# A fused linear-attention and gated-convolution kernel: query units over half the sequence, more transposing transfers, and a new written-out order

## The chip, the cores and the metric

The kernel runs on one core of a Trainium2 chip. The metric is device time in microseconds. The engines are TensorE (PE; its weight loads are listed apart as PEld), VectorE (DVE), ScalarE (ACT), GpSimd (POOL) and SyncE (SP, which here only issues transfers). Each engine takes its instructions strictly in order and waits for others on semaphores.

## The reference

Eight batches, eight heads, a sequence of 576, head size 64, 128 random features. Linear attention first, then a gated causal convolution block over the 512 columns that the heads make together:

```python
def phi(x):                                   # used for q and for k
    proj = np.einsum('bhsd,df->bhsf', x, w_phi)
    proj = proj - np.max(np.abs(proj), axis=-1, keepdims=True)
    return np.concatenate([np.exp(proj), np.exp(-proj)], axis=-1)
kv  = np.einsum('bhsf,bhsd->bhfd', k_p, v);   z = np.sum(k_p, axis=2)
num = np.einsum('bhsf,bhfd->bhsd', q_p, kv)
den = np.einsum('bhsf,bhf->bhs', q_p, z)[..., None] + 1e-06
x   = (num / den)                             # to [B, S, H*D]
for k in range(5):                            # causal: rows s-4 .. s
    gate_pre += conv_w[k] * xp[:, k:k + S, :]
out = (sigmoid(gate_pre) * (x @ w_val)) @ w_out
```

Inputs and output are float32; inside, the kernel works in bfloat16 with sums in float32 in PSUM.

## The kernel before

**Units.** For one batch, q (or k) is laid on 128 partitions with 18 blocks of 128 columns. A q partition stands for a head, a half of the sequence ("run", 288 rows) and one of eight places in it; a column block holds an even and an odd row of each partition. `UNITS` cuts the 18 blocks into four units of four blocks and one of two. Everything on k and q goes by unit: project (TensorE), take the maxima of the absolute values (VectorE, `amax`, L585), take both exponentials (ScalarE, `kexp` L595, `qexp` L706 and L709).

**One batch** runs through these steps, by the kinds that the plan gives them:

- `kp`, `kmax`, `kexp`: projected k, its maxima MK, the exponentials KTIL. `ek` makes EK from the maxima (ScalarE), and `vs` makes VT, v times EK (POOL, L610). `st` sums KTIL times VT over the sequence (TensorE, L620), `kv` evicts the sum.
- `qm`, `qmax`: projected q and its maxima MQP. `mqt` and `mqr` transpose and negate them to MQR. `rx` spreads MQR over an identity pattern to RX, so that a matmul with ones can subtract the maxima in PSUM. `qp` projects q again with features on partitions and adds RX (L693, L698); `qexp` writes QTIL.
- `num` (L719, L726), `nrm` (reciprocal and product, VectorE, L737 and L740, to XN), then the transpose of XN to XT: `xtp` on TensorE with the copy `xtc` (L748, L628/L632), or, for the batches in `XB`, a transposing transfer by SP (`xtd`, L755).
- `gate` (the convolution as matmuls, L781), `tanh` (ScalarE), `val` (L791), `gv` (VectorE, L797), `out` (L813, L817), `oev` (evict), `odma` (store).

**The start.** k and q of batch 0 come as float32 in nine loads by SP into the spare space of KTIL (`load32`); TensorE transposes them (`tp32`, L536) and ScalarE or VectorE casts them out of PSUM (`tc32`, L542, L544). Batch 1's k and q are loaded by POOL as bfloat16 and transposed on TensorE. From batch 2 on they are loaded by POOL and transposed by a transfer that SP issues (`xpose`, L565). `hold` is a tiny POOL copy that makes POOL's later loads wait for a first load of batch 0.

**The order.** Nothing is scheduled when the program is built. `build` lists 1062 tasks with their dependencies, and `ORDER` gives the order in which their instructions are written out; each engine runs its part of it in that order. `FLEX` says, for each task that has a choice of engine, which one it takes; `BANKS` gives the PSUM banks. `WARM` and `ZERO` put matmuls without use between tasks, to keep TensorE busy. The durations in `build` are the planner's own and play no part when the program runs.

Of the kernel before, what the change touches and what calls it, by code (L numbers as in the profile page):

```python
# [27 lines left out]
XB = (6, 7)  # L28
# [6 lines left out]
WARM = (  # L35
    "60:6:1 81:1:1 87:7:2 134:7:1 141:7:1 "
)
ZERO = "35:76:7 61:80:5 75:34:1 101:105:1 118:99:1 126:215:8 144:223:1 155:192:4 158:200:1 175:315:6 189:346:1 195:241:2 197:241:2 211:327:1"
# [41 lines left out]
)  # L80
FLEX = (
    "AAAAAADAAADDPPPPDDDDAADDDDDDDDDDDDDAAADAAAADDDDAAADDDAADAAADDADAADDDDADDDDADDDDDDAADADDAAAAAA"
)
BANKS = (
    "037362307001454523232323016701676714232367230101676012354423010145454501013660564675601456745010145450101676767014501454"
# [25 lines left out]
def dve(n, ov=0.075):  # L111
    return n / 960.0 + ov
# [50 lines left out]
def build(plan, em=None):  # L163
# [11 lines left out]
    def G(*k):  # L175
        return h.get(k)
# [3 lines left out]
    for b in range(B):  # L180

        if b == 0:
            last = A("lk", 0, 9, "SP", 0.3, None, rank=-1100)
            for w in "kq":
# [5 lines left out]
                if w == "q":  # L190
                    hold = [None, A("lk", b, 0, "POOL", 0.15, fn("hold", HOLDU), [lds[HOLDU]], rank=-600)]
# [709 lines left out]
```

## Time and profile before

| | |
|---|---|
| Time, median of 3 runs | 220.05 us (218.02 to 220.88) |
| Profiled execution, span from first to last instruction | 217.7 us |
| TensorE busy | 195.5 us, 90% |
| ScalarE busy | 180.8 us, 83% |
| VectorE busy | 170.2 us, 78% |
| POOL busy | 132.8 us, 61% |
| Granted TensorE clock, mean | 0.995 |

The profile comes from one execution; its page gives the span alone, and the timed runs lie 0.3 to 3.2 us over that span. "Busy" is the sum of instruction times; a busy TensorE is not TensorE at its peak, because matmuls overlap. In a row such as `L595 ACT ACTIVATE KTIL<-PS ... x64 | 63.5, 1050 | 2.6 <-DVE MK L585 1.3` stand the line, the engine, the operation, what it writes and reads, the count; then the busy microseconds and the mean nanoseconds of one; then the engine's idle time ahead of these instructions and what ended it. "issue" means that nothing in the profile explains the wait.

### The profile page before, as it was taken

The numbers are of one execution on the slowest core, as the hardware profiler recorded it, in microseconds if no ns is written. First come the engines' busy times: TensorE is split into PE (matmuls) and PEld (weight loads), VectorE is DVE, ScalarE is ACT, GpSimd is POOL, SyncE is SP. The second block draws the span as 40 slices with busy tenths as digits, with TensorE's granted clock in tenths as the row PEclk, the third lists the DMA queues.
The fourth block names the chain that finished last, engine by engine and source line by source line (L and its number), as shares of the span: only waits on it lengthen the run. The fifth ranks groups of instructions, "written<-read, shape, count | busy, mean of one in ns | idle before, by whom it ended". The sixth has DMA issues, their size and how long they took to land.

```text
span 217.7 us, 9029 instructions
## 1 busy us (share of the span) xinstructions
PE 195.5 (90%) x3946; PEld 138.6 (64%) x3946; DVE 170.2 (78%) x257; ACT 180.8 (83%) x267; POOL 132.8 (61%) x172
## 2 busy tenths in 40 slices
PE   2787887778999999998999999999999999899990
PEld 2555565566676676676857776567757766687740
DVE  3199979999789988997899978998699897654510
ACT  3589999999989899998999997999988988634251
POOL 3055999897793838970999089902993879210010
PEclk9999999999999999999999999999999999999997
DMA  6999998899899799989999778969953265764166
GB/s 177 364 234 215 302 188 231 149 174 199 144 152 284 139 135 213 302 154 174 233 276 168 88 165 248 190 142 203 287 183 89 63 160 128 81 168 97 48 186 202
DMA packets 49954, 39.92 MB, mean 183 GB/s; under 512 B 34165, under 2 KB 39541, under 8 KB 49914
## 3 DMA queue, kind: packets, MB, share of 16 engines
q1 hardware_dynamic: 43616, 28.65, 55.6%
q0 software_dynamic: 6032, 10.49, 26.3%
q8 instruction: 31, 0.51, 0.9%
q10 hardware_dynamic: 266, 0.21, 0.3%
q14 instruction: 9, 0.07, 0.1%
HBM read 30.48 MB, written 9.44 MB: 183 GB/s over the span
## 4 chain that ended last, share of the span: by engine, by line
PE 52%; ACT 23%; DVE 14%; DMA 5%; issue 4%; SPq 0%; DVEq 0%; ACTq 0%
PE PS L791 11%; ACT QTIL L706 9%; PE PS L781 9%; PE PS L813 9%; ACT KTIL L595 8%; DVE MQP L585 5%; PE PS L620 5%; PE PS L577 4%; PE PS L719 4%; DVE MK L585 3%; DMA KTIL<-in_k_dram 3%; PE PS L693 2%; DMA XT<-XN 2%; PE PS L817 2%; PE PS L698 2%
## 5 line engine op out<-in xcount | busy, mean ns | idle before, releaser
L595 ACT ACTIVATE KTIL<-PS 128x1024 bf16<-128x1024 f32 (+1 forms) x80 | 71.9, 960 | 4.1 <-PE PS L577 2.0
L610 POOL TENSOR_TENSOR VT<-VN,EK 128x1152 bf16<-128x1152 f32 x32 | 67.9, 2123 | 4.0 <-ACT EK L604 3.9
L706 ACT ACTIVATE QTIL<-PS 128x1024 bf16<-128x1024 f32 x64 | 62.5, 1044 | 2.4 <-PE PS L698 1.6
L682 POOL TENSOR_TENSOR RX<-MQR,ident 128x512 bf16<-128x512 bf16 (+1 forms) x39 | 36.6, 964 | 35.7 <-DVE MQR L670 26.0
L585 DVE TENSOR_REDUCE MK<-PS 128x8 f32<-128x1024 f32 (+1 forms) x40 | 44.2, 1112 | 2.9 <-PE PS L577 1.2
L585 DVE TENSOR_REDUCE MQP<-PS 128x8 bf16<-128x1024 f32 (+1 forms) x40 | 43.6, 1112 | 3.1 <-PE PS L577 2.3
L791 PE MATMUL PS<-XT,WV 128*128 128x288 bf16 x256 | 34.8, 286 | 0.3 <-DVE GV L797 0.2
L797 DVE SCALAR_TENSOR_TENSOR GV<-TH,PS 128x576 bf16<-128x576 bf16 x32 | 23.8, 752 | 10.4 <-PE PS L791 4.7
L813 PE MATMUL PS<-WOUT,GV 128*128 128x512 bf16 x128 | 31.3, 380 | 0.0
L791 PEld LDWEIGHTS <-WV 128*128 128x128 bf16 x256 | 23.8, 98 | 7.9 <-issue 1.4
L785 ACT ACTIVATE TH<-PS 128x576 bf16<-128x576 f32 x32 | 20.3, 663 | 9.5 <-PE PS L781 6.3
L620 PE MATMUL PS<-VT,KTIL 64*128 64x65 bf16 x1152 | 23.3, 191 | 1.1 <-issue 1.0
L781 PE MATMUL PS<-XT,GW 64*64 64x288 bf16 x640 | 23.1, 285 | 0.9 <-DMA XT<-XN 0.8
L740 DVE TENSOR_TENSOR XN<-PS,RCP 128x512 bf16<-128x512 f32 x32 | 22.1, 692 | 1.5 <-DMA XT<-XN 0.4
L620 PEld LDWEIGHTS <-KTIL 64*128 64x128 bf16 x1152 | 20.8, 94 | 3.8 <-issue 2.5
L719 PEld LDWEIGHTS <-QTIL 128*128 128x128 bf16 x512 | 18.3, 97 | 6.4 <-issue 4.0
L719 PE MATMUL PS<-KV,QTIL 128*128 128x65 bf16 x512 | 20.3, 194 | 0.3 <-DVE MQP L585 0.2
L781 PEld LDWEIGHTS <-GW 64*64 64x64 bf16 x640 | 17.8, 106 | 3.3 <-DVE RCP L737 0.9
L634 ACT ACTIVATE OUTS<-PS 128x512 f32<-128x512 f32 x22 | 13.5, 619 | 7.3 <-PE PS L813 6.1
L577 PE MATMUL PS<-W,qT 64*128 64x128 bf16 x288 | 15.1, 217 | 3.7 <-ACT qT L544 0.9
L813 PEld LDWEIGHTS <-GV 128*128 128x128 bf16 x128 | 11.1, 98 | 11.3 <-issue 0.6
L577 PEld LDWEIGHTS <-qT 64*128 64x128 bf16 x288 | 10.6, 94 | 10.3 <-issue 5.2
(79 smaller groups left out, 235.6 us busy)
## 6 DMA issues: line engine op xcount, KB each, us to landing
out_dram<-OUTS SPq DMA_DIRECT2D x32, 256.0 KB, 3.4
VN<-in_v_dram SPq DMA_DIRECT2D x7, 1152.0 KB, 6.3
KQN<-in_q_dram POOLq DMA_DIRECT2D x6, 576.0 KB, 8.3
KQN<-in_k_dram POOLq DMA_DIRECT2D x6, 576.0 KB, 9.8
KTIL<-in_k_dram SPq DMA_DIRECT2D x4, 288.0 KB, 4.5
VN<-in_v_dram POOLq DMA_DIRECT2D x1, 1152.0 KB, 10.6
KTIL<-in_q_dram SPq DMA_DIRECT2D x4, 256.0 KB, 5.7
out_dram<-OUTS SPq DMA_DIRECT2D x14, 64.0 KB, 2.6
```

What stands on the lines that cost most here:

```text
L577: nc.tensor.matmul(self.PS[:, t.grp.banks[par], i * P:(i + 1) * P], X[rows, (c0 + i) * P:(c0 + i + 1) * P], self.W2[rows, :], start=True, ...
L585: self.nc.vector.tensor_reduce(o, self.two(t.grp, n * P).rearrange("p a (c f) -> p a c f", f=F), AX.X, ALU.max, apply_absolute_value=True)
L595: self.nc.scalar.activation(self.KTIL[b % 2][:, s, c0:c0 + n, :, :].rearrange("p c a f -> p a c f"), self.two(t.grp, n * P).rearrange("p a ...
L610: nc.gpsimd.tensor_tensor(self.VT[g][:, s, :, 0:D], self.VN[b % 2][:, NC * g:NC * g + NC, :], e.to_broadcast([P, NC, D]), ALU.mult)
L620: nc.tensor.matmul(self.PS[:, t.grp.banks[ab], (s * 2 + x) * E1:(s * 2 + x + 1) * E1], self.KTIL[b % 2][rows, s, J // 2, J % 2, :], self.V ...
L682: self.nc.gpsimd.tensor_tensor(o, *wide(self.MQR[self.mq(b, u)][:, :], self.ident2), ALU.mult)
L706: self.nc.scalar.activation(o, i, AF.Exp, scale=1.0 - 2.0 * s)
L719: nc.tensor.matmul(self.PS[:, t.grp.banks[h // 4], (h % 4) * E1:(h % 4 + 1) * E1], Q[:, s, c % 2, h, (c // 2) * P:(c // 2 + 1) * P], self. ...
L781: self.nc.tensor.matmul(self.PS[o * D:(o + 1) * D, t.grp.banks[par], 0:R], self.GW[r, jj, 4 - m, :], X[r, 4 * a + jj, :, HALO - 8 * s:HALO ...
L791: self.nc.tensor.matmul(self.PS[:, t.grp.banks[par], 0:R], self.WV[:, i, (2 * j + par) * D:(2 * j + par + 2) * D], X[:, 4 * par + i, :, HA ...
L797: nc.vector.scalar_tensor_tensor(out=self.GV[b % 3][:, j, :, :], in0=self.TH[j][:, :, :], scalar=1.0, in1=self.two(t.grp, R), op0=ALU.add, ...
L813: nc.tensor.matmul(self.PS[:, t.grp.banks[0], :], GV[:, j, c % 2, (c // 2) * XH:(c // 2) * XH + P], self.WOUT[:, j, c % 2, :], start=(j == ...
```

## The change

1. **Units of q.** From `rx` and `qp` on, units 0 to 3 are no longer four column blocks over both runs, but eight column blocks (unit number modulo 2: blocks 0 to 7 or 8 to 15) over one run (unit number // 2). Unit 4 is as before. Sizes are the same. `QOF` and `QNEED` say which maxima and which transposed q they need. A numerator `num` for run 0 or 1 then waits for the two units of its run, and the last for unit 4, where all waited for all five units.
2. **Transposing transfers** of XN for batches 4 to 7 instead of 6 and 7.
3. **First loads.** The order of SP's loads is another, `hold` waits for all loads of k and q (it reads one element of each), and batch 1's v waits for it too. Batch 1 loads k ahead of q. `w_phi` comes in one transfer instead of two; the convolution weights are loaded by SP behind the first loads, instead of by ScalarE's queue ahead of everything.
4. **Choice of engine.** `vs`, and `rx` of all batches, may go to VectorE. In the new `FLEX` all `vs` stay on POOL, and 12 of 40 `rx` go to VectorE (before: one).
5. **A new ORDER, FLEX, BANKS, WARM and ZERO**, made by a planner that reckons with the time in which an engine's instructions are fetched. The filling matmuls go from 158 to 72.

```diff
-XB = (6, 7)
+QOF = {(0, 1): (0, 2), (2, 3, 4): (1, 3, 4), (0, 1, 2, 3, 4): (0, 1, 2, 3, 4)}
+QNEED = ((0, 1), (2, 3), (0, 1), (2, 3), (4,))
+XB = (4, 5, 6, 7)
...
-ZERO = "35:76:7 61:80:5 75:34:1 101:105:1 118:99:1 126:215:8 144:223:1 155:192:4 158:200:1 175:315:6 189:346:1 195:241:2 197:241:2 211:327:1"
+WARM = "94:4:1 105:0:2 143:0:1 162:0:3 215:6:1 300:5:1 306:4:1"
+ZERO = "70:50:6 86:93:1 230:350:5 327:449:4"
...
-                    hold = [None, A("lk", b, 0, "POOL", 0.15, fn("hold", HOLDU), [lds[HOLDU]], rank=-600)]
+                    hold = [None, A("lk", b, 0, "POOL", 0.15, fn("hold", HOLDU), lds + klds, rank=-600)]
...
-            for w in "qk":
+            for w in "kq" if b == 1 else "qk":
...
+            cl = A("lk", 0, 0, "SP", 0.5, fn("c_cwl"), [])
+            cl = A("lk", 0, 0, "DMA", 3.0, None, [cl])
+            cc = A("mqt", 0, 0, "PE", 0.5, fn("c_cw"), [G("tp", "q", 1), cl], g, rank=-500)
...
-                h["vs", b, gi, s] = A("vs", b, gi, "POOL", 2.22, fn("vs", b, gi, s),
+                h["vs", b, gi, s] = A("vs", b, gi, ("POOL", "DVE"), (2.22, 1.36), fn("vs", b, gi, s),
...
-            for u in us:
+            for u in QOF[us]:
...
-            qp = h["qp", b, u] = A("qp", b, u, "PE", 0.118 * n, fn("qp", b, u), [rx, G("xq", b, u)], g, 1)
+            qp = h["qp", b, u] = A("qp", b, u, "PE", 0.118 * n, fn("qp", b, u), [rx] + [G("xq", b, y) for y in QNEED[u]], g, 1)
...
-            num = h["num", b, c] = A("num", b, c, "PE", 0.57 if c < 4 else 0.38, fn("num", b, c), allq,
+            need = [G("qexp", b, u, s) for u in ((2 * (c // 2), 2 * (c // 2) + 1) if c < 4 else (4,)) for s in range(2)]
+            num = h["num", b, c] = A("num", b, c, "PE", 0.57 if c < 4 else 0.38, fn("num", b, c), need + [G("kv", b, i) for i in range(2)],
...
-        for i in range(2):
-            nc.scalar.dma_start(self.W32[i * D:(i + 1) * D, :], self.wphi[:, :])
+        nc.scalar.dma_start(self.W32[:, :], self.wphi[:, :].unsqueeze(0).to_broadcast([2, D, F]))
         nc.vector.tensor_copy(self.W2[:, :], self.W32[:, :])
-        nc.scalar.dma_start(self.cw5[:, :], self.wts[1][:, :])
...
-        o = self.RX[u][:, :, 0:n, :]
+        o = self.RX[u][:, 0:nh * ny * 8].rearrange("p (h y x) -> p h y x", h=nh, y=ny)
...
+            else:
+                self.nc.vector.tensor_tensor(o, *wide(self.MQR[mq][:, :], self.ident2), ALU.mult)
+
+    def qys(self, u):
+        return (8 * (u % 2), 8) if u < 4 else UNITS[4]
...
-            o = self.QTIL[b % 2][:, s, :, :, :].rearrange("p a h (k r) -> p a (h k) r", k=2)[:, :, :, u * 32:(u + 1) * 32]
-            self.nc.scalar.activation(o, i, AF.Exp, scale=1.0 - 2.0 * s)
+            self.nc.scalar.activation(self.QTIL[b % 2][:, s, :, :, u * D:(u + 1) * D],
+                                      self.two(t.grp, n * P).rearrange("p a (h r) -> p a h r", h=H), AF.Exp, scale=1.0 - 2.0 * s)
```

What the new order does on an engine is not in these lines. Three places show it. First, ScalarE from its first cast on (kT and qT are the transposed k and q of batch 0, KTIL the exponentials of k). Before:

```order
L544 CAST kT_68<-PS 128x512 x3
L595 ACTIVATE KTIL_72<-PS 128x2x4x128 x2
L544 CAST qT_70<-PS 128x512
L595 ACTIVATE KTIL_72<-PS 128x2x4x128
L544 CAST kT_68<-PS 128x512
L595 ACTIVATE KTIL_72<-PS 128x2x4x128 x2
```

And now:

```order
L550 CAST kT_68<-PS 128x512
L601 ACTIVATE KTIL_72<-PS 128x2x4x128 x2
L550 CAST qT_70<-PS 128x512
L601 ACTIVATE KTIL_72<-PS 128x2x4x128
L550 CAST kT_68<-PS 128x256
L601 ACTIVATE KTIL_72<-PS 128x2x4x128
L550 CAST qT_70<-PS 128x512
```

The first two exponentials stand behind one cast instead of three; two casts of kT went to VectorE.

Second, VectorE in batch 3, from the negated maxima (MQR) on. Before:

```order
L670 TENSOR_SCALAR MQR_91<-PS 128x128
L585 TENSOR_REDUCE MK_85<-PS 128x2x4
L630 TENSOR_SCALAR OUTS_114<-PS 128x512
L797 SCALAR_TENSOR_TENSOR GV_107<-TH_102,PS 128x576
L737 RECIPROCAL RCP_96<-PS 128x8
L740 TENSOR_TENSOR XN_97<-PS,RCP_96 128x512
```

And now:

```order
L677 TENSOR_SCALAR MQR_91<-PS 128x128
L815 SCALAR_TENSOR_TENSOR GV_107<-TH_102,PS 128x576
L591 TENSOR_REDUCE MK_85<-PS 128x2x4
L637 TENSOR_SCALAR OUTS_114<-PS 128x512
L637 TENSOR_SCALAR OUTS_112<-PS 128x512
L698 TENSOR_TENSOR RX_137<-MQR_91,ident_130 128x512
L698 TENSOR_TENSOR RX_134<-MQR_91,ident_130 128x512
L635 CAST KV_93<-PS 128x520
L698 TENSOR_TENSOR RX_138<-MQR_91,ident_130 128x256
```

Three of the batch's five RX are now made here, with both inputs (MQR and the identity pattern) in SBUF; before, POOL made all five.

Third, SP around the transposing transfers of batch 7's k and q (kT_69, qT_71). Before:

```order
L836 DMA out_dram<-OUTS_111 16x2x512 x4
L531 DMA VN_66<-in_v_dram 128x4x576
L830 DMA out_dram<-OUTS_112 16x8x512
L565 DMA_TRANSPOSE kT_69<-KQN_64 128x18x128
L565 DMA_TRANSPOSE qT_71<-KQN_65 128x18x128
L830 DMA out_dram<-OUTS_118 16x8x512
```

And now:

```order
L848 DMA out_dram<-OUTS_116 16x8x512
L773 DMA_TRANSPOSE XT_100<-XN_97 128x8x128
L773 DMA_TRANSPOSE XT_100<-XN_98 128x8x128
L571 DMA_TRANSPOSE kT_69<-KQN_64 128x18x128
L571 DMA_TRANSPOSE qT_71<-KQN_65 128x18x128
L848 DMA out_dram<-OUTS_115 16x8x512
L537 DMA VN_66<-in_v_dram 128x4x576
L773 DMA_TRANSPOSE XT_101<-XN_98 128x8x128
```

The two transfers that transpose XN of batch 4 stand ahead of them, and the first of batch 5's follows three places behind.

More of the change, by code (lines that the diff above doesn't have):

```diff
@@ L256, in build @@
         ld = h["lv0",] = A("lv", b, 0, "POOL" if b == 1 else "SP", 0.65, fn("loadv", b),
-               [G("vs", b - 2, g, s) for g in range(2) for s in range(2)] + [G("lv0",) if b > 2 else None],
+               [G("vs", b - 2, g, s) for g in range(2) for s in range(2)] + [G("lv0",) if b > 2 else hold[1] if b == 1 else None],
                rank=-980 if b == 0 else None)
@@ L298, in build @@
             mqr = A("mqr", b, i, "DVE", dve(128), fn("mqr", b, i), [mqt] + [G("rx", b - 2, u) for u in range(NU)], gm)
-            for u in us:
+            for u in QOF[us]:
                 n = UNITS[u][1]
-                h["rx", b, u] = A("rx", b, u, ("POOL", "DVE") if b == 0 else "POOL", (0.35 * n - 0.1, dve(n * P)) if b == 0 else 0.35 * n - 0.1,
+                h["rx", b, u] = A("rx", b, u, ("POOL", "DVE"), (0.35 * n - 0.1, dve(n * P)),
                                   fn("rx", b, u, i), [mqr, G("qp", b - 1, u)], gm if b == 0 else None)
@@ L393, in __init__ @@
             self.N[w][1] = spare[:, i * NR:(i + 1) * NR].rearrange("p (y c) -> p y c", c=2 * D)
-        self.HOLD = T("HOLD", [P, 1])
+        self.HOLD = T("HOLD", [P, 2, 9])
         self.ONES = T("ONES", [P, 512])
@@ L429, in __init__ @@
         nc.vector.tensor_scalar(self.nident2[:, :], self.ID2[:, :], -1.0, None, op0=ALU.mult)
-        self.RX = TT("RX", NU, [P, 2 * H, 4, 8])
+        self.RX = TT("RX", NU, [P, 4 * P])
         self.WV = T("WV", [P, 4, DM + D])
@@ L507, in hold @@
     def hold(self, t, u):
-        c = UNITS[u][0] * P
-        self.nc.gpsimd.tensor_copy(self.HOLD[:, :], self.XN32["q"][:, c:c + 1])
+        x = self.KTIL[1][:, :, :, :, :].rearrange("p s c a f -> p s (c a f)").bitcast(FP32)
+        self.nc.gpsimd.tensor_copy(self.HOLD[:, :, :], x.rearrange("p s (u x) -> p s u x", x=256)[:, :, :, 0])
     def holdx(self, t, b):
-        self.nc.gpsimd.tensor_copy(self.HOLD[:, :], self.XT_["q"][b % 2][:, NR - 1:NR])
+        self.nc.gpsimd.tensor_copy(self.HOLD[:, 0, 0:1], self.XT_["q"][b % 2][:, NR - 1:NR])
     def rows(self, w, b):
@@ L692, in qp @@
             rows = slice(par * D, (par + 1) * D)
-            nc.tensor.matmul(self.PS[:, t.grp.banks[par], 0:n * P], self.W2[rows, :],
-                             X[rows, c0 * P:(c0 + n) * P].rearrange("p (y h x) -> p h y x", y=n, h=2 * H),
+            m = X[rows, y0 * P:(y0 + ny) * P]
+            m = m.rearrange("p (y h k x) -> p h k y x", y=ny, h=H, k=2)[:, :, u // 2] if u < 4 else m.rearrange("p (y h x) -> p h y x", y=ny, h=2 * H)
+            nc.tensor.matmul(self.PS[:, t.grp.banks[par], 0:w], self.W2[rows, :], m,
                              start=True, stop=True, skip_group_check=True)
@@ L697, in qp @@
             rows = slice(par * D, (par + 1) * D)
-            nc.tensor.matmul(self.PS[:, t.grp.banks[par], 0:n * P].rearrange("p (h y x) -> p h y x", h=2 * H, y=n),
-                             self.ONES[rows, 0:F], self.RX[u][rows, :, 0:n, :], start=False, stop=True, skip_group_check=True)
+            nc.tensor.matmul(self.PS[:, t.grp.banks[par], 0:w], self.ONES[rows, 0:F], self.RX[u][rows, 0:w],
+                             start=False, stop=True, skip_group_check=True)
     def qexp(self, t, b, u, s):
         c0, n = UNITS[u]
-        i = self.two(t.grp, n * P).rearrange("p a (h r) -> p a h r", h=2 * H)
         if u < 4:
-            o = self.QTIL[b % 2][:, s, :, :, :].rearrange("p a h (k r) -> p a (h k) r", k=2)[:, :, :, u * 32:(u + 1) * 32]
-            self.nc.scalar.activation(o, i, AF.Exp, scale=1.0 - 2.0 * s)
+            self.nc.scalar.activation(self.QTIL[b % 2][:, s, :, :, u * D:(u + 1) * D],
+                                      self.two(t.grp, n * P).rearrange("p a (h r) -> p a h r", h=H), AF.Exp, scale=1.0 - 2.0 * s)
         else:
+            i = self.two(t.grp, n * P).rearrange("p a (h r) -> p a h r", h=2 * H)
             for a in range(2):
```

46 lines of the change are left out of this document (26 added, 20 removed), and 72 rows, old and new, of the table ORDER.

## The prediction

> **What bounds the kernel now.** I read the busy times by stage first, because one mean over the whole span hides that the limits change. The columns are the busy time of each engine, then the granted clock, the DMA share and GB/s.
>
> ```profile
> core 0: us, PE busy (x) PEld busy (x) DVE busy (x) ACT busy (x) POOL busy (x), PEclk, DMA share, GB/s
> 0.00:9.20 9.20, 4.13 (x29) 3.02 (x30) 2.00 (x6) 3.04 (x4) 1.78 (x12) 1.00 0.80 246
> 9.20:20.00 10.80, 8.53 (x125) 6.40 (x125) 9.32 (x10) 10.13 (x15) 5.68 (x8) 1.00 1.08 255
> 20.00:100.00 80.00, 71.59 (x1651) 51.78 (x1654) 70.69 (x105) 76.88 (x112) 62.17 (x70) 1.00 0.97 198
> 100.00:188.00 88.00, 87.51 (x1809) 60.79 (x1798) 77.51 (x119) 80.08 (x119) 60.98 (x74) 1.00 0.79 170
> 188.00:212.50 24.50, 23.73 (x347) 16.62 (x345) 10.73 (x20) 10.03 (x17) 2.19 (x8) 1.00 0.50 126
> 212.50:217.70 5.20, 0.02 (x2) 0.00 (x0) 0.00 (x0) 0.60 (x1) 0.00 (x0) 0.77 0.62 198
> ```
>
> Four stages. Until 9.2 us the first loads set the pace. From 20 to 100 us ScalarE is the fullest engine (76.88 of 80); TensorE has 8.4 us without a matmul and VectorE 9.3 us without work. From 100 to 212.5 us TensorE is never out of work (87.51 of 88, then 23.73 of 24.5), and what ScalarE leaves over is worth nothing there. The last 5.2 us are one eviction and the final stores.
>
> The chain that ended last, asked for 20 to 100 us alone, agrees: exponentials first, then the maxima on VectorE.
>
> ```profile
> by line: ACT QTIL L706 18.1%; ACT KTIL L595 14.4%; DVE MQP L585 12.1%; PE PS L620 6.5%; PE PS L781 5.0%; DVE MK L585 4.6%; issue 4.5%; PE PS L577 4.5%; DVE XN L740 3.6%; ACT QTT L709 3.2%; PE PS L791 2.8%; DVE GV L797 2.7%; ACT TH L785 2.1%
> ```
>
> VectorE's four entries make 23% of it (12.1 + 4.6 + 3.6 + 2.7). So an edit counts if it starts the exponentials earlier, takes VectorE or ScalarE work out of the first hundred microseconds, or takes TensorE work out of the rest.
>
> **The start.** Rows of the timeline, in order of time:
>
> ```profile
> 4.97 0.59 ACT L544 CAST kT<-PS 128x512 bf16<-128x512 f32 x1 [0.93 <-PE PS L536]
> 5.29 0.23 DVE L455 CAST W<-W 128x128 bf16<-128x128 f32 x1 [2.48 <-DMA W<-in_w_phi_dram]
> 7.29 0.90 PE L536 MATMUL PS<-ident_f,KTIL 128*128 128x128 f32 x3 [1.21 <-DMA KTIL<-in_k_dram]
> 8.13 1.04 PE L577 MATMUL PS<-W,kT 64*128 64x128 bf16 x16
> 9.21 1.94 ACT L595 ACTIVATE KTIL<-PS 128x1024 bf16<-128x1024 f32 x2 [0.39 <-PE PS L577]
> 11.01 0.19 POOL L509 CAST HOLD<-KTIL 128x1 bf16<-128x1 f32 x1 [8.62 <-DMA KTIL<-in_q_dram]
> ```
>
> Before, the first projection stands on TensorE behind the transposes of the third k load, which landed at 7.29. In the new order it stands behind the first k load alone. Its inputs are there when the cast of kT (4.97 + 0.59 = 5.56) and of W (5.29 + 0.23 = 5.52) are done; eight of the sixteen matmuls of 1.04 us take a little over half of that, and the first exponential can start at about 6.3 instead of 9.2. That is 2.9 us at most. The last of the first loads still lands around 11.0. By then ScalarE had done three casts and two exponentials (3 x 0.59 + 1.94 = 3.7 us); now it can have done a cast and what fits from 6.3 to 11.0, 5.3 us. It is 1.6 us ahead at that point. Bounds 1.6 and 2.9; I take **2.0**, near the lower, since the second half of each load set is no earlier. ScalarE paces the stage that follows, so TensorE is full that much sooner.
>
> The new wait on all first loads stands ahead of batch 1's loads on POOL. The HOLD row shows that POOL already waited for the last q load until 11.01, which was issued behind all of k. So it costs 0, at most the 0.4 us of one more issue on SP. The convolution weights, loaded later, are wanted only after the first q transposes: 0.
>
> **Transposing transfers for batches 4 and 5.** Four groups of eight TensorE transposes go, with their copies. Two groups on the chain, one copy group, and the price of a transfer in their place:
>
> ```profile
> 95.91 0.89 PE PS L748 x16
> L628 DVE COPY XT<-PS 128x1024 bf16<-128x1024 bf16 x10 | 6.7, 680 | 0.0
> 185.71 4.54 DMA XT<-XN
> 190.38 2.03 PE PS L781 x60
>   PE PS L781: 0.8, 1
> ```
>
> Sixteen transposes take 0.89 us, so 32 take **1.8 us**, all in the stage where TensorE is full: there it comes off the end one for one. The four copies that go stand beside a full TensorE and give 0. The transfers take 4.54 us from the normalized rows to the gate matmuls; in the batches that had them TensorE waited for one of the four, 0.8 us (the last row: wait and times), because other batches' matmuls stood between. If that cover is missing for all four, 3.2 us come back. On SP, whose queue runs in order, two of them now stand ahead of the transposes of batch 7's k and q. Durations on SP (min/median/max ns), and first and last start:
>
> ```profile
> L755 SPq DMA_TRANSPOSE XT<-XN x4: 1231/1273/2017, 181.7 to 194.6; - x4
> L565 SPq DMA_TRANSPOSE qT<-KQN x6: 2691/3217/3502, 30.1 to 146.8; - x6
> ```
>
> Two issues are 2.5 us, by which batch 7's q, issued at 146.8, can come later. TensorE is full there with other batches' matmuls, so I take 0; it costs up to 2.5 if those run out.
>
> **Reductions of the maxima moved from POOL to VectorE.** RX is built on VectorE 12 times instead of once: 6 of 128x512 and 6 of 128x256. Rows by shape:
>
> ```profile
> L682 POOL TENSOR_TENSOR RX<-MQR,ident 128x512 bf16<-128x512 bf16 x32 | 32.6, 1040 | 35.7 <-DVE MQR L670 26.0 <-DVE RCP L737 6.6 <-DVE MQR L667 3.1
> L740 DVE TENSOR_TENSOR XN<-PS,RCP 128x512 bf16<-128x512 f32 x32 | 22.1, 692 | 1.5 <-DMA XT<-XN 0.4
> L685 DVE TENSOR_TENSOR RX<-PS,nident 128x256 bf16<-128x256 bf16 x1 | 0.4, 415 | 0.0
> L542 DVE CAST qT<-PS 128x512 bf16<-128x512 f32 x1 | 0.7, 692 | 4.8 <-ACT KTIL L595 4.8
> L610 POOL TENSOR_TENSOR VT<-VN,EK 128x1152 bf16<-128x1152 f32 x32 | 67.9, 2123 | 4.0 <-ACT EK L604 3.9
> ```
>
> Batches 0 to 3 get five of 0.69 and two of 0.42 more: 4.3 us into a stage where VectorE idles 9.3 us. (The two casts more at the start, 0.69 each, lie where VectorE waited 4.8 us ahead of its first one: 0.) POOL waits 35.7 us ahead of its own RX, so POOL's relief gives nothing by itself; an RX gets shorter by 1040 - 692 = 0.35 us, and no longer stands behind a VT of 2.12 us. Bounds: 0 (hidden in the idle time) and 4.3 (all on the path). VectorE had 23% of the chain there; I take 23% of 4.3, **1.0 us** lost.
>
> **Refills of instructions.** The page puts 3.9% of the chain down to "issue". Most of it is no stop. The first row is from the chain, the second is the timeline of ScalarE over the same time:
>
> ```profile
> 110.81 0.60 issue
> 110.49 3.79 ACT L706 ACTIVATE QTIL<-PS 128x1024 bf16<-128x1024 f32 x4
> ```
>
> ScalarE works straight through that "issue". On TensorE I find one true stop (chain rows, then the queue that loads instructions: packets, MB, share):
>
> ```profile
> 97.36 0.68 PE PS L620 x41
> 98.03 0.96 issue
> 99.00 0.68 PE PS L620 x26
> q8 instruction: 31, 0.51, 0.9%
> ```
>
> An order that places such stops elsewhere can win 0.96 us at most, 0 at least; I take half, **0.5 us**, since both orders cross equally many blocks. The Trainium skill's page "Runtime: NRT & Kernel Launch", section "Instruction fetch mechanics", holds that fetching is hidden, since instructions are dispatched more slowly than they are filled in. By it this term would be 0; the row of 0.96 us speaks against it, once in 31 refills.
>
> **The rest at nothing.** Query exponentials now write runs of 64 instead of 32; those of k, with runs of 128, take the same:
>
> ```profile
> L595 ACT ACTIVATE KTIL<-PS 128x1024 bf16<-128x1024 f32 x64 | 63.5, 1050 | 2.6 <-DVE MK L585 1.3 <-PE PS L577 0.6 <-DVE GV L797 0.3
> L706 ACT ACTIVATE QTIL<-PS 128x1024 bf16<-128x1024 f32 x64 | 62.5, 1044 | 2.4 <-PE PS L698 1.6 <-PE PS L504 0.6
> L504 PE MATMUL PS<-ONES,NIL 64*128 64x128 bf16 x140 | 5.6, 216 | 0.0
> ```
>
> Ninety of the 152 filling matmuls go; they stood in TensorE's holes of the first 60 us, and the clock is 1.00 even in the first stage, where TensorE is 45% busy. That numerators need two units instead of five lets TensorE begin them earlier, which is worth something only before 100 us: 0 to the 8.4 us idle there. I take 0, because ScalarE stays at 96% in that stage and the sum of exponentials is unchanged.
>
> **Sum.** 217.7 - 2.0 - 1.8 - 0.5 + 1.0 = 214.4 us of span. The profiled span lies 2.35 us under the median of the runs, 220.05, of which part lies around the span and part is how runs differ; I add it back: **216.8 us**.
>
> **Rivals.** First, **the front half closes up**: half of TensorE's 8.4 us there is won by the earlier numerators, and VectorE's 4.3 us stay hidden. 217.7 - 2.0 - 1.8 - 0.5 - 4.2 = 209.2, or 211.6 us. For it: the numerators were the last work of a batch that waited for all ten exponentials. Against it: ScalarE has 3.1 us to give in that stage.
>
> Second, **VectorE becomes the bound of the front half, or the transfers come late**. With all 4.3 us on the path: 217.7 - 4.3 + 4.3 = 217.7, or 220.1 us; with four waits of 0.8 us on top, 223.3. For it: VectorE would be at 94% from 20 to 100 us ((70.69 + 4.3) / 80). This is also the case in which the refills are not placed any better.
>
> Third, on the other side, **RX on VectorE is held up by POOL**. The same cast of 128x128 took, while POOL ran its memsets, and later while POOL did not:
>
> ```profile
> L418 DVE CAST ident<-ident_f 128x128 bf16<-128x128 f32 x1 | 1.0, 987 | 0.1
> L455 DVE CAST W<-W 128x128 bf16<-128x128 f32 x1 | 0.2, 229 | 2.5 <-DMA W<-in_w_phi_dram 2.5
> ```
>
> VectorE can lose 0.76 us beside POOL. Ten of the new RX read both inputs from SBUF, six of them before 100 us, where POOL is 78% busy, mostly with VT. A wait of half a VT (1.06 us) in 78% of six cases is 5.0 us. VectorE's remaining idle time is 9.3 - 4.3 = 5.0 us, so it decides once these RX are longer by 0.83 us each (5.0 / 6), those of 128x512 over 1.5 us. Then all of it is on the path: 217.7 - 4.3 + 4.3 + 5.0 = 222.7, or 225.1 us. The Trainium skill's page "SBUF — State Buffer", section "Who interferes with whom", says that a VectorE instruction with two SBUF inputs and a GpSimd instruction that reads SBUF lock each other out. No run here shows that case yet.
>
> **How the numbers follow.** Forecast 0.38, with 214.5 to 219.5 as its own range; closing up 0.24 (209 to 214.5); VectorE bound or late transfers 0.22 (219.5 to 224); POOL's hold 0.16 (224 to 229). A measurement of this kernel can tell about 2% from no change, 4.4 us. Under 215.65 lie the 0.24 and a fifth of the forecast, 0.32; over 224.45 lies most of the last, 0.15; between them 0.53. For 8 in 10 I leave out the lower end of the closing up and the upper two thirds of POOL's hold: 211 to 225 us.
>
> **What would show it.** First exponential at 6 to 7 us: the start term. TensorE full from about 97 us, with fewer transposes: the second. VectorE from 20 to 100 us at 75 us or more, with RX at 0.69: the fourth; RX over 1.5: the third rival. No row of TensorE with "issue" near 0.9: the refills. The forecast is wrong if TensorE is full much earlier than 95 us, or has holes after 110 us at the gates of batches 4 and 5.

## The result and the profile after

The changed kernel takes 240.81 us (median of four, 238.88 to 245.54) against 219.73 us (218.02 to 220.88) of the kernel before in the same session: 1.094 times as long, 95% interval 1.085 to 1.104. The forecast was 216.8, with 225 as the end of its range. The profiled execution has a span of 237.1 us, 19.4 more than that of before. Where the runs of a kernel fell into two groups, the ratios use the faster group alone, and the one profile that is of a slower run (the old order with transposing transfers in four batches) is not read here.

First the page of the changed kernel: TensorE's busy time over the span, then 40 slices of 5.9 us each with the busy tenths of three engines and the granted clock.

```profile
PE 197.7 (83%) x3808; PEld 135.5 (57%) x3828; DVE 184.7 (78%) x267; ACT 180.5 (76%) x264; POOL 125.3 (53%) x161
PE   3978668239859999878899899989999999999980
DVE  3799998997939979999898689878989776743520
POOL 3185997940676501698598345930479894010000
PEclk9999997956999999999999999999999999999998
```

In the 8th and 9th slice (41 to 53 us) TensorE drops to 2 and 3 tenths while VectorE counts as nine tenths busy, POOL too in the first of them, and the clock goes to half behind it. By stages, in the same form as in the prediction (the windows of before, then of after):

```profile
10.00:40.00 30.00, 24.57 (x527) 17.66 (x526) 27.34 (x35) 28.22 (x44) 22.99 (x26) 1.00 1.03 234
40.00:60.00 20.00, 16.66 (x423) 12.30 (x419) 17.41 (x27) 19.24 (x28) 17.09 (x19) 1.00 0.95 168
60.00:150.00 90.00, 87.61 (x1866) 62.06 (x1862) 81.18 (x123) 85.28 (x125) 60.08 (x77) 1.00 0.94 191
```

```profile
10.00:40.00 30.00, 22.89 (x456) 16.57 (x457) 28.85 (x40) 29.16 (x46) 23.61 (x27) 0.95 0.99 213
40.00:60.00 20.00, 10.40 (x203) 8.14 (x203) 17.86 (x17) 10.86 (x16) 10.36 (x11) 0.74 0.88 149
60.00:150.00 90.00, 81.15 (x1689) 55.71 (x1699) 77.62 (x118) 79.35 (x117) 54.66 (x69) 1.00 0.79 174
```

Between 40 and 60 us TensorE loses 6.3 us of busy time and a quarter of its clock; from 60 to 150 us it loses another 6.5 us. The prediction had expected a net gain in both stages. The first loss has one instruction behind it. The timeline of VectorE and of POOL at that place, and the next matmul on TensorE (start, us, engine, line, operation, and in brackets the wait ahead of it and what ended it):

```profile
40.70 0.69 DVE L758 TENSOR_TENSOR XN<-PS,RCP 128x512 bf16<-128x512 f32 x1
41.31 8.49 DVE L698 TENSOR_TENSOR RX<-MQR,ident 128x512 bf16<-128x512 bf16 x1
49.73 0.19 DVE L755 RECIPROCAL RCP<-PS 128x8 f32<-128x8 f32 x1
```

```profile
40.49 2.15 POOL L617 TENSOR_TENSOR VT<-VN,EK 128x1152 bf16<-128x1152 f32 x1
42.56 0.28 POOL L618 CAST VT<-EK 128x18 bf16<-128x18 f32 x1
...
47.14 2.11 POOL L617 TENSOR_TENSOR VT<-VN,EK 128x1152 bf16<-128x1152 f32 x1
49.20 0.71 POOL L618 CAST VT<-EK 128x18 bf16<-128x18 f32 x1
```

```profile
50.70 0.61 PE L712 MATMUL PS<-qT,W 64*128 64x512 bf16 x2 [7.62 <-DVE XN L758]
```

An RX of 128x512, 0.68 us elsewhere on VectorE, took 8.49 us. It began while POOL ran the first of four VT, and it ended 0.55 us after the last of the four did (49.25 to 49.80). That last row of POOL, a cast of 0.26 us elsewhere, took 0.71 us: it is the first that was itself held. Everything behind RX on VectorE waited, and TensorE stood for 7.62 us.

The second loss has many small parts; the largest are stops for which the profile shows no releaser. The largest waits of TensorE from 60 to 150 us (us in total, times, longest):

```profile
PE PS L799 <- issue: 2.5, 1, 2.5
PE PS L627 <- issue: 0.8, 1, 0.8
PE PS L770 <- DVE XNT L758: 0.5, 2, 0.4
```

The start did what it was to do: the first exponential ran at 6.47 us, after 9.21 us before.

```profile
6.47 1.94 ACT L601 ACTIVATE KTIL<-PS 128x1024 bf16<-128x1024 f32 x2 [1.02 <-PE PS L583]
```

### The profile page after: what moved, and what is told of

Same layout as the page of the kernel before. It is cut to its first block, busy times and chain, and to the rows that moved or that the text cites. A ratio compares the mean times of both kernels' runs of the same rounds, so it can differ in the third digit from the quotient of the medians.

```text
span 237.1 us, 8755 instructions
## 1 busy us (share of the span) xinstructions
PE 197.7 (83%) x3808; PEld 135.5 (57%) x3828; DVE 184.7 (78%) x267; ACT 180.5 (76%) x264; POOL 125.3 (53%) x161
## 4 chain that ended last, share of the span: by engine, by line
PE 53%; DVE 25%; ACT 7%; issue 6%; DMA 5%; SPq 0%; DVEq 0%; ACTq 0%
PE PS L809 12%; PE PS L831 9%; PE PS L799 8%; DVE MQP L591 6%; PE PS L583 5%; DVE MK L591 5%; PE PS L737 5%; PE PS L627 4%; DVE XN L758 4%; DVE RX L698 4%; ACT KTIL L601 3%; PE PS L712 3%; DMA XT<-XN 2%; PE PS L716 2%; DVE GV L815 2%
## 5 line engine op out<-in xcount | busy, mean ns | idle before, releaser
L692 POOL TENSOR_TENSOR RX<-MQR,ident 128x512 bf16<-128x512 bf16 (+1 forms) x28 | 28.4, 1028 | 29.7 <-DVE MQR L677 25.7
L809 PE MATMUL PS<-XT,WV 128*128 128x288 bf16 x256 | 35.8, 286 | 2.0 <-issue 1.1
L831 PE MATMUL PS<-WOUT,GV 128*128 128x512 bf16 x112 | 29.9, 379 | 0.9
L799 PE MATMUL PS<-XT,GW 64*64 64x288 bf16 x640 | 24.3, 286 | 3.1 <-issue 2.5
L627 PEld LDWEIGHTS <-KTIL 64*128 64x128 bf16 x1152 | 21.5, 96 | 6.5 <-issue 3.9
L712 PE MATMUL PS<-qT,W 64*128 64x512 bf16 (+1 forms) x80 | 15.6, 375 | 10.1 <-DVE XN L758 8.0
L799 PEld LDWEIGHTS <-GW 64*64 64x64 bf16 x640 | 17.2, 106 | 8.2 <-issue 6.3
L831 PEld LDWEIGHTS <-GV 128*128 128x128 bf16 x128 | 11.3, 97 | 12.1 <-issue 1.2
L583 PE MATMUL PS<-W,kT 64*128 64x128 bf16 x288 | 15.3, 224 | 3.2 <-ACT KTIL L601 0.9
```

The costliest lines, as they stand in the source:

```text
L627: nc.tensor.matmul(self.PS[:, t.grp.banks[ab], (s * 2 + x) * E1:(s * 2 + x + 1) * E1], self.KTIL[b % 2][rows, s, J // 2, J % 2, :], self.V ...
L692: self.nc.gpsimd.tensor_tensor(o, *wide(self.MQR[mq][:, :], self.ident2), ALU.mult)
L799: self.nc.tensor.matmul(self.PS[o * D:(o + 1) * D, t.grp.banks[par], 0:R], self.GW[r, jj, 4 - m, :], X[r, 4 * a + jj, :, HALO - 8 * s:HALO ...
L809: self.nc.tensor.matmul(self.PS[:, t.grp.banks[par], 0:R], self.WV[:, i, (2 * j + par) * D:(2 * j + par + 2) * D], X[:, 4 * par + i, :, HA ...
L831: nc.tensor.matmul(self.PS[:, t.grp.banks[0], :], GV[:, j, c % 2, (c // 2) * XH:(c // 2) * XH + P], self.WOUT[:, j, c % 2, :], start=(j == ...
```

## The experiments

### Is it the place of that RX, or too much work on VectorE

The changed kernel, with one number moved in its order, so that this RX stands ahead of the chain of VT and stays on VectorE:

```diff
-    "... 332 206 318 234 331 426 ... 433 239 "
-    "231 122 434 ... "
+    "... 332 206 231 318 234 331 426 ... 433 239 "
+    "122 434 ... "
```

> The changed kernel with one VectorE instruction moved: the 128x512 RX of batch 1 that took 8.49 us at 41.31 stands four VectorE instructions and some 3 us earlier, ahead of the chain of VT scalings on POOL, and stays on VectorE. Theory A (that RX was held by the POOL instructions running beside it): it takes 0.68 us, the TensorE stop of 7.62 us before the matmul at 50.70 and the clock of 0.5 at 47.0 to 57.3 go, and the kernel comes to 227 to 233 us (from 240.8; 8 to 13 us less). Rival B (VectorE has too much to do, and the long row only shows where it was waited for): the time stays within 2 us of 240.8, and another VectorE row becomes the one waited for.

Measured: 235.84 us, 1.079 times before (1.070 to 1.087). That is 3.5 us (by the ratios) to 5.0 us (by the medians) less than the change: about half of what theory A said, and more than rival B allowed. The trace shows what held the time up (VectorE, then TensorE):

```profile
39.23 0.68 DVE L698 TENSOR_TENSOR RX<-MQR,ident 128x512 bf16<-128x512 bf16 x1
45.20 4.55 DVE L698 TENSOR_TENSOR RX<-MQR,ident 128x256 bf16<-128x256 bf16 x1
```

```profile
50.93 0.40 PE L583 MATMUL PS<-W,qT 64*128 64x128 bf16 x8 [4.80 <-DVE MQP L591]
```

The moved RX took its 0.68 us. The next RX of batch 1, a 128x256 one of 0.41 us that used to come after the chain, now came at 45.20, inside it, and was held until the fourth VT ended, 4.55 us; TensorE stood 4.80 us. So VectorE's load is not the matter: the same RX takes 8.49 or 0.68 us by what POOL does beside it.

### All RX of batches 1 to 7 back on POOL, or only those of batch 1

```diff
             t.eng = names[f]
+            if t.kind == "rx" and t.b:         # the second kernel: t.b == 1
+                t.eng = "POOL"
```

> The changed kernel with all RX of batches 1 to 7 back on POOL, ten instructions, order unchanged. Theory A: no RX is longer than 1.1 us; the three that ran beside POOL (8.49, 1.22, 1.30 us) are no longer held; 226 to 232 us. Were it that POOL and VectorE share nothing and only the work counts, VectorE would lose ten instructions of 0.41 to 0.68 us, 6 us of its 148, and the kernel would gain 2 us at most: 238 to 241 us. In both, what stays above 219.7 us is not due to RX but to the rest of the change (order, fillers, transfers).

> The changed kernel with only batch 1's two RX on POOL; the other eight on VectorE as in the change. Theory A'' (only the chain of batch 1 holds an RX through; the rest costs nothing): the same as with all ten on POOL, 228 to 231 us. Rival (each RX on VectorE costs, 1.22 and 1.30 us of two of them beside POOL): 231 to 235.

Measured: 229.34 us with all ten, 1.046 times before (1.036 to 1.056); 231.83 us with batch 1's two only, 1.056 (1.050 to 1.063). Against the change's 1.094, ten RX on VectorE cost 4.9% or some 11 us, and batch 1's two alone 3.8% or 8 us. Between the two kernels lies 1%, and their intervals overlap, so the other eight cost some 2 us (231.83 lies in the rival's range) and perhaps nothing. Theory A holds for batch 1. And 4.6% of loss stays without RX of these batches on VectorE: about half of the question is still open after this.

### What lets VectorE in: one RX beside another chain of VT

In the kernel before, one RX of batch 7 was put on VectorE, with both inputs in SBUF as in the change, at a place where POOL's four VT of that batch run:

```diff
+        for t in self.tasks:
+            if (t.kind, t.b, t.u) == ("rx", 7, 2):
+                t.eng = "DVE"
```

> The kernel before with one RX, the 128x512 one of batch 7 unit 2, on VectorE instead of POOL. It stands among VectorE's work at about 178.4 us, where POOL runs four VT scalings one behind the other (176.6 to 185.5 in the trace of before). Theory A: it takes until that chain ends, 5 to 7 us instead of 0.68, and the kernel comes to 223 to 228 us. Theory A' (it waits for the one POOL instruction that runs as it comes, then goes first): 1 to 2.9 us, kernel 219 to 222. Rival B: 0.68 to 0.7 us, kernel 219 to 221.

Measured: 219.59 us, 1.003 times before (1.000 to 1.007). VectorE's row, and POOL's:

```profile
178.83 0.87 DVE L689 TENSOR_TENSOR RX<-MQR,ident 128x512 bf16<-128x512 bf16 x1
```

```profile
177.04 2.12 POOL L613 TENSOR_TENSOR VT<-VN,EK 128x1152 bf16<-128x1152 f32 x1 [0.99 <-ACT EK L607]
179.10 0.73 POOL L614 CAST VT<-EK 128x18 bf16<-128x18 f32 x1
```

RX came into the first VT, waited until that VT ended, and ran; now POOL's cast was the one held, 0.73 us instead of 0.27. So theory A in its plain form, that a queued chain of POOL keeps VectorE out until it has run dry, falls here. A' has the mechanism right; RX came 0.3 us before the VT ended, so the price is 0.2 us, less than the range of A'.

To see more cases, all RX of batches 1 to 7 were put on VectorE (the same two lines as above with "DVE"), for one look:

> The changed kernel with all 38 RX of batches 1 to 7 on VectorE, order unchanged: one look at many RX beside POOL's work. Theory A (an RX waits until POOL's queued chain has run out): RX that arrive within a chain of VT scalings take 3 to 8.8 us, wherever the chain is; 250 to 275 us. Theory A' (it waits for the instruction that POOL is in, and is let in at its end): none over 3.0 us; 240 to 250 us. Between the two (a chain lets it in at some ends of instructions and not at others, as the trace with RX moved early against before's batch 7 suggests): some over 4 us, and some under 2.5 us that arrived in a chain; then what stands ahead of each chain on POOL is compared.

It took 251.97 us in its one run. Four of its RX that came while a VT ran:

```profile
44.27 7.72 DVE L700 TENSOR_TENSOR RX<-MQR,ident 128x512 bf16<-128x512 bf16 x1
125.99 1.86 DVE L700 TENSOR_TENSOR RX<-MQR,ident 128x512 bf16<-128x512 bf16 x1
183.06 2.27 DVE L700 TENSOR_TENSOR RX<-MQR,ident 128x512 bf16<-128x512 bf16 x1
204.35 2.16 DVE L700 TENSOR_TENSOR RX<-MQR,ident 128x512 bf16<-128x512 bf16 x1
```

The case between the two came out. In three chains RX was let in at the end of the VT that ran; in batch 1's it was held again until the fourth VT had ended. In the three kernels that had an RX there, it was held through two VT or more each time. What sets that chain apart is what stands ahead of it. In the change POOL waits for qT, issues three transfers from 38.4 to 40.5 us, and only then begins the VT, whose last input (EK) had been ready since 38.3:

```profile
38.28 0.19 POOL L518 COPY HOLD<-qT 128x1 bf16<-128x1 bf16 x1 [1.51 <-DMA qT<-KQN]
38.41 0.80 POOL L471 DMA_DIRECT2D WOUT<-in_moe_w_out_dram  x1
39.20 0.55 POOL L556 DMA_DIRECT2D KQN<-in_q_dram  x1
39.74 0.76 POOL L556 DMA_DIRECT2D KQN<-in_k_dram  x1
```

Two issues of transfers alone are not enough. In the run with all RX on VectorE, two of them stand right ahead of the chain in which the RX at 125.99 was let in at the first end. There the last input of the VT, v, landed at 125.0, during the second issue:

```profile
123.79 0.60 POOL L558 DMA_DIRECT2D KQN<-in_q_dram  x1
124.39 0.75 POOL L558 DMA_DIRECT2D KQN<-in_k_dram  x1
125.15 2.14 POOL L619 TENSOR_TENSOR VT<-VN,EK 128x1152 bf16<-128x1152 f32 x1
127.22 0.75 POOL L620 CAST VT<-EK 128x18 bf16<-128x18 f32 x1
```

As a test, the four instructions ahead of batch 1's chain (that wait and the three issues) were moved behind it, and RX left where the change has it:

```diff
-    "... 331 426 427 236 352 353 108 428 431 235 237 109 432 433 239 231 122 434 208 ... 210 213 327 ..."
+    "... 331 236 352 353 108 235 237 109 239 231 122 208 ... 210 213 426 427 428 431 432 433 434 327 ..."
```

> The changed kernel as it is, but four POOL instructions (the one that waits for qT, and three DMA issues: WOUT and q and k of batch 3) stand behind the chain of four VT scalings of batch 1 instead of ahead of it; RX of batch 1 stays on VectorE beside that chain. Theory Q (POOL keeps VectorE out over a whole chain only where its instructions were all queued and ready while it issued DMAs): RX is let in at the end of the VT or the cast that runs as it comes, 0.8 to 2.9 us instead of 8.49; 228 to 235 us. Rival (something else in this chain): RX takes until the end of the fourth VT again, 5 to 8.5 us; 238 to 244 us.

Measured, in one run: 236.64 us. VectorE's two RX of batch 1, POOL's instructions at the first of them, and a later stop of TensorE:

```profile
42.48 0.90 DVE L698 TENSOR_TENSOR RX<-MQR,ident 128x512 bf16<-128x512 bf16 x1
44.97 0.81 DVE L698 TENSOR_TENSOR RX<-MQR,ident 128x256 bf16<-128x256 bf16 x1
```

```profile
40.71 2.12 POOL L617 TENSOR_TENSOR VT<-VN,EK 128x1152 bf16<-128x1152 f32 x1
42.77 0.73 POOL L618 CAST VT<-EK 128x18 bf16<-128x18 f32 x1
```

```profile
65.57 0.40 PE L583 MATMUL PS<-W,kT 64*128 64x128 bf16 x4 [4.71 <-DMA kT<-KQN]
```

The durations are theory Q's: 0.90 us instead of 8.49, and 0.81 for the other, each let in at the end of the VT that ran as it came. The chain and the RX are the same. What differs is what stands ahead of the chain, and with it that the chain begins at 38.50 instead of 40.49, so that the first RX comes into its second VT instead of its first. The time, 236.64, is over theory Q's range: the loads of batch 3, issued 10 us later, were late for TensorE, which stood 4.71 us at 60.9 and paid back what was won. Why a chain that was ready behind issues of transfers keeps the next engine out over several of its instructions is not settled by this. That what stands ahead decides it rests on this one run; whether it is the number of issues (three against two) or how long before their end the inputs were there (1.4 to 2.7 us in the three kernels, 0.2 at 125.15) was not tried.

### Is the rest in the new code or in the order

The changed functions with the numbers of the kernel before: its order, engines, banks and fillers, carried over task by task, and transposing transfers in batches 6 and 7 only. A second kernel has them in 4 to 7, as the change does:

```diff
-XB = (4, 5, 6, 7)
+XB = (6, 7)                      # the second kernel: (4, 5, 6, 7)
-ORDER, FLEX, BANKS, WARM, ZERO as in the change
+ORDER, FLEX, BANKS, WARM, ZERO as in the kernel before
```

> The changed kernel's functions (half-run query units, first loads all awaited, one transfer for W, cw5 on SP, k of batch 1 loaded first, transposing transfers in batches 6 and 7 only) with the numbers of the kernel before: its ORDER, engine choices, banks and fillers, carried over task by task; three tasks move, since the new units need more than the old ones. Theory D (what is left of the loss after RX is the order itself): 216 to 220 us. Theory E (the new units, whose operands are read with other strides, or the later loads of batch 1 cost the time): 224 to 230 us.

> The same with transposing transfers in batches 4 to 7, as in the change; what differs from the run with them in 6 and 7 is this alone: 32 transposes and four copies out of PSUM fall away, four transfers are added. The prediction's step: 1 to 2 us less than that run. Rival (the gates of batches 4 and 5 wait for transfers that take 5.2 us from issue to landing in the trace of after): 1 to 4 us more.

Measured: 220.2 us, 1.009 times before (1.005 to 1.013); and 224.54 us, 1.029 (1.024 to 1.034). The first is theory D, 0.2 us over its range: the half-run units, the wait on all first loads, the single transfer of W and the loads' new turn cost about 1%, 1.3% at most. Between it and the kernel with RX on POOL (1.046) lie 3.7%, 8 to 9 us: the order with its engine choices, banks and fillers, and two more batches of transposing transfers. The second kernel is on the rival's side of the prediction's step: put into the order of before, these two batches of transfers cost 2%, where the prediction had them save 1.8 us.

For the new order the reverse was tried: RX on POOL, and batches 4 and 5 of XT on TensorE again.

```diff
-XB = (4, 5, 6, 7)
+XB = (6, 7)                      # and four banks, free at these places, in BANKS
```

> The changed kernel with RX of batches 1 to 7 on POOL (229.3 us) and, on top, batches 4 and 5 of XT transposed on TensorE again, as before, in four free banks of PSUM. Theory F (the added transposing transfers cost in any order; in the order of before they brought 4.3 us): 224 to 227 us. Prediction's step (they save 1.8 us of TensorE): 230 to 232 us.

Measured: 1.057 times before (1.049 to 1.065, from two of its four runs), some 232 us, against 1.046 (1.036 to 1.056) without it. The time did not come down to the 224 to 227 us of theory F, but the run is not clean: the copies out of PSUM were put in by hand between tasks that were planned without them, and at 136.2 us TensorE stood 1.80 us for one of them. Whether the transfers save anything in the new order stays open. Two things speak against them as the source of its loss: taking them back won nothing, and in the traces of the change and of the kernel with RX on POOL no row of TensorE's waits is for a transferred XT (before: one of 0.8 us).

### The fillers

```diff
+        warm, zero = {}, {}
         for i, t in enumerate(plan.follow()):
```

> The kernel before without its 152 filling matmuls, which compute nothing that is read; all else unchanged. The prediction's step (the fillers cost nothing and bring nothing; the granted clock stays 1.00 without them): 219 to 221 us and a clock of 1.0 up to 200 us. Theory C (the fillers hold the granted clock up through the waits of the first 60 us): stretches of 3.4 to 10 us at 0.5 appear before 60 us, each of which costs about half its length in TensorE work: 223 to 229 us.

Measured: 222.72 us, 1.017 times before (1.009 to 1.025). That is over the prediction's range and 0.3 us under theory C's. The clock's row on the page of this kernel:

```profile
PEclk9997699999999999999999999999999999999998
```

It falls to half from 19.4 to 26.2 us, where it had stayed at full speed with the fillers: theory C's mechanism, at less than its lowest price. This profile is of the shortest run (220.92 us, mean clock 0.98); the other three took 222.7 to 222.8 at 0.95 to 0.96.

### The end

In the kernel with RX on POOL, the shared output unit of batches 6 and 7 was moved behind all others, as in the kernel before (two transfers of 64 KB at the end, instead of one of 256 KB):

```diff
-    "... 1041 809 804 931 805 932 1058 927 933 796 1054 797 928 1059 929 1062 1060 1046 ... 1044 1045 "
+    "... 1041 809 804 931 805 932 927 933 796 1054 797 928 929 1046 ... 1044 1045 1058 1059 1062 1060 1061 1063 "
```

> The changed kernel with RX of batches 1 to 7 on POOL, and the shared last output unit of batches 6 and 7 (two transfers of 64 KB) put last, as in the kernel before, instead of a unit whose transfer is 256 KB; in the traces 5.2 us lie between the last matmul and the end of the span of before and 7.2 in this one. Theory G (the end waits for the longer transfer): 1.5 to 2.2 us less than 229.3, so 227 to 228. Rival (the end is set by transfers queued on SP in any case): 229 to 230.

Measured: 1.042 times before (1.032 to 1.052), against 1.046 (1.036 to 1.056): no difference that can be told, and theory G's 1.5 to 2.2 us would hardly show in such intervals. The traces decide: here 7.0 us still lie between the last matmul and the end, after 7.1. Theory G falls. A likely reason is that SP had 17 output transfers to issue after 205 us in the new order and 9 before, and that evictions waited for free output buffers (0.83 us at one, 2.75 at another); that was not tried.

## Why the prediction was wrong

**What bounds the kernel.** The stages were read rightly for before. But the forecast treated each stage's slack as there to be used. Two steps failed most. RX on VectorE stood in the sum at 1.0 us and cost some 11: one instruction stopped two engines in the front half. The new order stood at nothing and cost, with what came with it, 8 to 9: it leaves TensorE without work in the stage where it had no time to spare.

**The start, -2.0.** Right in place and size: the first exponential came 2.74 us earlier (bound 2.9), and TensorE's first projection 2.3 us earlier. What failed is the step behind it, "ScalarE paces the stage that follows, so TensorE is full that much sooner". Count TensorE's matmuls without fillers and transposes, each at its mean time in the kernel before. The kernel with RX on POOL had a tenth of them done at 43.5 us, the kernel before at 46.4; a fifth of them at 67.4 and 66.9. So the lead reached TensorE, and was spent between 44 and 67 us. (The busy time from 10 to 40 us, 21.77 us after 24.57, hides the lead: 3.31 and 7.75 us of it are filling matmuls.)

**RX on VectorE, +1.0, with 0 to 4.3.** This is the term that was mis-sized most: some 11 us by the run without it, and some 8 of them for batch 1 alone. The third rival named the mechanism and the place (an RX held by POOL, before 100 us) and the sign by which it would show, "RX over 1.5". It priced it as half a VT for each of six RX, 5.0 us, with a chance of 0.16. The runs show two cases instead: let in at the end of the instruction that runs, 0.2 to 1.6 us each and hardly a cost; or held over a chain, 8.49 us once. A mean wait over all RX prices neither. The profile of before held a better bound: the longest run of POOL instructions without a gap, 8.9 us for four VT and their casts, and whoever waits behind VectorE for that long. The Trainium skill's page "SBUF — State Buffer", section "Who interferes with whom", calls the port between the two engines an exclusive lock and has two SBUF inputs on VectorE contend with POOL's reads. All these rows agree that one engine waits for the other's instruction to end; that the lock can pass from one POOL instruction to the next six times over, as in the 8.49 us, is not in it.

**Refills, -0.5, with 0 to -0.96.** Wrong in sign. TensorE's waits from 60 to 150 us in the kernel before, and then the largest in the new order with RX on POOL, which has the new order's stops without the hold:

```profile
PE PS L620 <- issue: 1.0, 1, 1.0
PE PS L791 <- DVE GV L797: 0.2, 1, 0.2
PE PS L577 <- issue: 0.2, 1, 0.2
```

```profile
PE PS L811 <- issue: 1.8, 1, 1.8
PE PS L629 <- issue: 1.1, 1, 1.1
PE PS L772 <- DVE XNT L760: 0.5, 2, 0.4
PE PS L739 <- DVE MQP L593: 0.5, 1, 0.5
```

The longest stop has an instruction transfer beside it, as the 0.96 us had before: one began at 143.72 and TensorE stood from 144.50 to 146.25. At that very matmul, the 118th of the values, six kernels of the new order stood 0.94 to 2.01 us (the change 1.14, and 2.50 at another transfer, at 65.8); the one with all RX on VectorE did not stand there, but 1.73 and 2.82 us elsewhere. "Both orders cross equally many blocks" was true (30 and 31) and said nothing, because the price of a block is not fixed. The Trainium skill's page "Runtime: NRT & Kernel Launch", section "Instruction fetch mechanics", holds that fetching is mostly hidden; for most of the transfers the traces agree, for these rows they don't. (The second rival says that refills are no better in its case, and still has the 0.5 us in its sum; without it 220.1 would be 220.6 us.) All this is read from traces, and that the transfers cause these stops is inferred from their place; no run moved the refills alone.

**Fillers, at nothing.** The step "the clock is 1.00 even in the first stage, where TensorE is 45% busy" took the first 9 us, where the clock is 1.00 and no filler stands, for the whole front. All fillers of the kernel before stand from 10 to 60 us, and without them it lost 1.7%, with the clock at half from 19.4 us on. In the new order the clock also fell after long stops. The windows of after behind the held RX, and of the kernel with RX on POOL behind its stop of 1.75 us:

```profile
47.00:57.30 10.30, 5.65 (x106) 4.86 (x107) 8.46 (x10) 4.07 (x7) 3.36 (x6) 0.50 0.69 119
```

```profile
146.50:149.90 3.40, 3.40 (x79) 2.60 (x77) 2.59 (x3) 0.84 (x1) 0.00 (x0) 0.50 1.16 92
```

The clock is the number behind the five busy times. At half clock this kernel's matmuls of the values start 240 ns apart, elsewhere 122. So where TensorE is full, 3.4 us at half speed cost 1.7 us of work, and that stop of 1.75 us cost twice its length. Not every such stop did: the one of 2.50 us in the change kept the clock at 1.00.

**The order, at nothing.** No term stood for it. The prediction priced the edits and took the new order as neutral between them. That was the largest omission beside RX: with the order of before the changed code takes 220.2 us, with its own and RX on POOL 229.34 (and two more batches of transposing transfers). The spans of these two kernels (217.3 and 228.6) are 11.3 us apart: 9.3 at the last matmul, and 2.0 more behind it (7.1 after 5.1). By the same count of matmuls as above, the new order has a tenth of them done 3.5 us earlier than the old one and a fifth at the same time (67.4 and 67.2 us). It has half of them done 4.7 us later and 60% 9.0 us later (150.1 and 141.1), and from there on the distance stays. So the loss arises between 67 and 150 us. From 60 to 150 us TensorE is idle for 7.6 us after 2.2, of which the stops for instructions are 2.9 us after 0.6; it spends 1.4 us on filling matmuls after none, and the half clock costs 1.7. This is an account of two traces, of which the second is of the longest of its four runs (230.34 us), not a test of each part. What the 86 filling matmuls fewer of the new order cost in it was not tried. The rows, first the old order's and then the new one's:

```profile
60.00:150.00 90.00, 87.85 (x1870) 61.81 (x1862) 81.27 (x123) 85.22 (x127) 60.35 (x77) 1.00 0.98 191
```

```profile
10.00:40.00 30.00, 21.77 (x450) 15.33 (x447) 28.13 (x39) 28.73 (x46) 22.85 (x26) 1.00 1.04 213
60.00:150.00 90.00, 82.42 (x1703) 55.62 (x1702) 75.48 (x111) 79.77 (x114) 62.55 (x76) 0.98 0.94 183
```

**Transposing transfers, -1.8.** TensorE's 32 transposes did go. In the order of before they brought 2% more instead, which is the second rival's side; that its late transfers are the reason was not shown. In the new order it stays open whether they save anything.

**The signs named ahead.** The first held (first exponential at 6.47); RX over 1.5, the sign of the third rival, came with the 8.49 us. The holes after 110 us at the gates of batches 4 and 5 did not come: no wait of TensorE was for a transferred XT. "TensorE full from about 97 us" failed, and so did the sign of no TensorE row with "issue" near 0.9; both tell of the loss of the second half.

## What to carry to other kernels

When a VectorE instruction gets two SBUF inputs, look in the trace for the longest unbroken run of POOL beside its place, and price that run for everything that waits behind VectorE, not a mean wait; if it must stand there, see that POOL doesn't come to its chain with all of it ready behind a few issues of transfers (one run here speaks for that). Price a new order on its own: put the old order under the new code, and the new one under the old choices, before the edits are added up. And where TensorE is full, a stop of about 2 us may cost twice its length, since the clock can follow it.

## What the runs showed of the hardware

- A POOL instruction and a VectorE instruction with both inputs in SBUF take turns at ends of instructions, in both directions: RX waited for VT (0.87 to 2.27 us instead of 0.68), and then POOL's cast waited for RX (0.71 to 0.75 us instead of 0.27). RX that read PSUM, beside a POOL RX (in the change) or a VT (before, 22.68 us), took its usual 0.41 and 0.68 us.
- Behind three issues of transfers, POOL's chain of VT let VectorE in only after the fourth VT, in all three kernels that had an RX there (8.49, 4.55, 7.72 us); with the issues behind the chain it let it in at the first end (0.90 and 0.81 us). Behind two issues, with the last input landing during the second, it let it in at the first end too (1.86 us).
- The granted clock fell to 0.50, for 3.4 us or two or three times that, with stops of TensorE of 1.75, 1.80, 1.94, 2.01, 4.71, 4.80, 6.08 and 7.62 us, and began within the stop or up to 1.5 us after its end. After stops of 1.73 (two kernels), 1.82, 1.87, 2.50 and 2.82 us it stayed at 1.00. What tells the two groups apart was not found. Before 50 us, where TensorE works in short pieces, it fell in some executions without such a stop (36.8 to 40.2 in the change).
- Of some 30 instruction transfers in a run, on the queue whose transfers lie beside TensorE's stops, most passed without a stop; at the one matmul where six kernels stood, the stop's length differed from kernel to kernel (0.94 to 2.01 us).
